# Prologue of a fused attention and MLP block: modulation products ahead of the transposes, weights by chunk, dummies gated by statistics

## Chip, cores, metric

One core of a Trainium2 chip. The metric is the device time of one execution, in microseconds; the kernel before has a median of 560.35 us in the first three runs (560.24 to 560.86). A trace shows one profiled execution, and "span" is the time from its first to its last instruction, about 1.8 us less than the device time. "PE" is the matmul engine, "PEld" its weight loads, "DVE", "ACT" and "POOL" the vector, scalar and GpSimd engines, "SP" the sync queue.

## The reference, cut

```python
mod = (silu(c) @ w_mod).reshape(1, 6, 1, -1)
sa, ca, ga, sb, cb, gb = ...                        # six rows of 512
h = layernorm(x) * (1 + ca) + sa                    # x: 2048 x 512
x = x + ga * attention(h @ wq, k_cache, v_cache) @ wo    # 32 query heads, the last 512 keys
h = layernorm(x) * (1 + cb) + sb
x = x + gb * (relu(h @ w1) @ w2)
```

Everything is bf16. Before the first attention unit the kernel needs the first 512 rows of x normalised and transposed, silu(c), the two rows sa and ca as columns, and the query weights of two heads.

## The kernel before

The parts that the change touches, all in the prologue ("tile" is 128 rows of x). Later on, 128 units of scores, softmax, values and projections run on PE without a pause.

```python
    for i in range(2):
        dma(x_sb[:, 2 * i:2 * i + 2, :], ..., eng=ACT if i else SP)      # x, tiles 0-1 and 2-3
    dma(c_row[:, :], ...)
    load_wm01(0)                 # first half of the weights of sa, ca: SP
    load_wm01(1, ACT)            # second half
    load_wq(0, 2, ACT)           # query weights of heads 0 and 1
    load_wq(2, 2)
    load_k(0)
    load_v(0)
    kb.op(POOL, lambda e: e.memset(ones[:, :], 1.0), writes=[R_ones])
    ...
    warm(7)                      # dummies: matmuls ones x ones, 512 columns
    silu_exp(5)                  # transpose of c on PE, exp and copy on ACT
    warm(9)
    ...                          # ACT: sum and square of tile 3
    silu_mul()                   # POOL: 1/(1+exp(-c)), times c
    ln_stat(0)                   # DVE: mean and variance
    ln_stat(1)
    rstd_add(0, 2)
    rstd_pow(0, 2)               # POOL
    ln_stat(2)
    rstd_add(2, 3)
    rstd_pow(2, 4)               # POOL
    ln_norm(0)                   # DVE
    ln_norm(1)
    kb.op(POOL, ... xn[:, t3, :] ...)     # tile 3 is normalised on POOL
    ...
    ln_tposes(0, TB[0])          # four PE transposes of tile 0
    fs = mod_cols_mm(0, QBK)     # 32 products w_mod column block x silu(c)
    for f in fs:
        f()
    ln_norm(2)
    mod_cols_evac(0, QBK)        # DVE: modc, the columns of sa and 1 + ca
    ...
    for tl in range(1, TPB):
        ln_tposes(tl, TB[tl // 2])
    mod_half(0, 0, DVE)          # hT = transposed tile * (1 + ca) + sa
    ...
    q_half(0, 0, CC_ORDER, QBK)  # query projection, half a block at a time
```

Near the end, each engine reads a flag (is every softmax sum in range?) and branches past a slow fallback program:

```python
                v = e.value_load(flag[0:1, 0:1])
                with e.If(v != 128):
                    ...                        # the fallback
                with e.Else():
                    kb.emit(stream, e, n_ops)  # the rest of the fast path
```

Of the kernel before, what the change touches and what calls it, by code (L numbers as in the profile page):

```python
# [128 lines left out]
def all_events(res_list):  # L129
    evs = []  # L130
    for r in res_list:
        if r.w is not None:
            evs.append(r.w)
        evs.extend(r.r)
    return evs
# [1063 lines left out]
def build_fast(nc, es, top, A_x, A_k_cache, A_v_cache, A_wq, A_wo, B_x, B_w1, B_w2, c, w_mod, out, flag):  # L1199
    P = 128  # L1200
    _, Sq, D = A_x.shape
    _, G, Sk, Dh = A_k_cache.shape
# [5 lines left out]
    QB = 512  # L1208
    NB = Sq // QB
    TPB = QB // P  # L1210
    NT = Sq // P
    DC = D // P
# [15 lines left out]
    def T(name, shape, dt=BF):  # L1228
        return es.enter_context(nc.sbuf_tensor(name, shape, dt))
# [3 lines left out]
    wq_sb = wq_t[:, :].rearrange("p (c n) -> p c n", c=DC)  # L1233
# [12 lines left out]
    wm01 = wmw[:, 0:2 * DC * D].rearrange("p (c n) -> p c n", c=DC)  # L1246
    wm = [wm01[:, :, 0:D], wm01[:, :, D:2 * D]] + [wmw[:, i * DC * D:(i + 1) * DC * D].rearrange("p (c n) -> p c n", c=DC) for i in range(2, 6)]
# [8 lines left out]
    ones = T("ones", [P, P])  # L1256
# [25 lines left out]
    bank = [s_ps[0][:, 0, :], s_ps[0][:, 1, :], s_ps[1][:, 0, :], s_ps[1][:, 1, :], q_ps[:, :],  # L1282
            o_ps[:, 0:2, :].rearrange("p a b -> p (a b)"), o_ps[:, 2:4, :].rearrange("p a b -> p (a b)"), w_ps[:, :]]
    QBK, WBK = 4, 7

    sem = lambda name: top.enter_context(nc.semaphore(name))
    kb = KB(nc)
    PE = kb.stream("pe", sem("s_pe"))
    ACT = kb.stream("act", sem("s_act"))
    DVE = kb.stream("dve", sem("s_dve"))  # L1290
    POOL = kb.stream("pool", sem("s_pool"))
    SP = kb.stream("sp", sem("s_sp"))

    def dsem(key):
        if key not in kb.dma_cnt:
            kb.add_dma_sem(key, sem("d_" + key))
        return key

    def dma(out_ap, in_ap, key, reads=(), writes=(), transpose=False, eng=None):
        k = dsem(key)  # L1300
        if transpose:
            return kb.op(SP, lambda e: e.dma_start_transpose(out_ap, in_ap), reads=reads, writes=writes, dma_sem=k)
        return kb.op(eng or SP, lambda e: e.dma_start(out_ap, in_ap), reads=reads, writes=writes, dma_sem=k)  # L1303

    RL = lambda name, n: [Res(f"{name}{i}") for i in range(n)]
    R_x, R_wq, R_wo = RL("x", NT), RL("wq", H), RL("wo", NPASS)
    R_kT, R_v, R_v1 = RL("kT", G), RL("v", G), Res("v1")
    R_hT, R_h2T = [RL(f"hT{i}_", DC) for i in range(2)], [RL(f"h2T{i}_", DC) for i in range(2)]
    R_qT, R_PT, R_o, R_oT = RL("qT", NQT), [RL(f"PT{i}_", 2) for i in range(NPT)], RL("o", NOS), RL("oT", NOT)
    R_acc, R_wm, R_w1, R_w2 = RL("acc", TPB), RL("wm", 6), RL("w1", FC), RL("w2", FC)  # L1310
# [3 lines left out]
    R_ident, R_ones, R_c, R_sc, R_scf, R_tmp, R_cst = (Res(n) for n in ("ident", "ones", "c", "sc", "scf", "tmp", "cst"))  # L1314
    R_moda, R_modb, R_ga, R_gb = Res("moda"), Res("modb"), Res("ga"), Res("gb")
    R_pr = [R_ga] + RL("pr", 2) + [R_gb]
    R_st, R_mv, R_rstd = RL("st", NT), RL("mv", NT), RL("rstd", NT)
    R_h0 = RL("h0", DC)
    R_q1 = RL("q1_", 2)
    R_cf, R_m01 = Res("cf"), Res("m01")  # L1320
    R_s3, R_eps = Res("s3"), Res("eps")
    R_rinv, R_vmax, R_chk, R_good, R_flag = Res("rinv"), Res("vmax"), Res("chk"), Res("good"), Res("flag")
# [4 lines left out]
    wqv = A_wq.rearrange("(c p) n -> p c n", p=P)  # L1327
# [8 lines left out]
    def load_wq(h0, n, eng=None):  # L1336
        dma(wq_sb[:, :, h0 * Dh:(h0 + n) * Dh], wqv[:, :, h0 * Dh:(h0 + n) * Dh], f"wq{h0}", writes=R_wq[h0:h0 + n], eng=eng)

    def load_k(g):
        dma(kT_sb[:, g, :], A_k_cache[0][g, Sk - W:, :], f"k{g}", writes=[R_kT[g]], transpose=True)  # L1340
# [7 lines left out]
    wm01v = w_mod[:, 0:2 * D].rearrange("(c p) n -> p c n", p=P)  # L1348

    def load_wm01(i, eng=None):  # L1350
        c0, c1 = i * DC // 2, (i + 1) * DC // 2
        dma(wm01[:, c0:c1, :], wm01v[:, c0:c1, :], f"wm{i}", writes=[R_wm[i]], eng=eng)

    def wm_res(sl, cc):
        return R_wm[cc // (DC // 2)] if sl < 2 else R_wm[sl]

    def load_wo(j):
        dma(wo_sb[:, j * HQ:(j + 1) * HQ, :], wov[:, j * HQ:(j + 1) * HQ, :], f"wo{j}", writes=[R_wo[j]])
# [1 line left out]
    wm_done = []  # L1360

    def load_mlp(i):
        if not wm_done:
            wm_done.extend(all_events(R_wm))
        f0 = i % (FC // 2) * 2
        if i < FC // 2:
            kb.op(SP, lambda e: e.dma_start(w1_sb[:, :, f0 * P:(f0 + 2) * P], w1v[:, :, f0 * P:(f0 + 2) * P]), writes=R_w1[f0:f0 + 2], pre=wm_done, dma_sem=dsem(f"w1{f0}"))
        else:
            kb.op(SP, lambda e: e.dma_start(w2_sb[:, f0:f0 + 2, :], w2v[:, f0:f0 + 2, :]), writes=R_w2[f0:f0 + 2], pre=wm_done, dma_sem=dsem(f"w2{f0}"))

    def mm(out_ap, lhsT, rhs, start, stop, reads, bk, signal):
        kb.op(PE, lambda e: e.matmul(out_ap, lhsT, rhs, start=start, stop=stop), reads=reads, group_writes=[R_b[k] for k in bk], signal=signal)  # L1372
# [1 line left out]
    def tpose(out_ap, in_ap, reads, bk, signal):  # L1374
        kb.op(PE, lambda e: e.transpose(out_ap, in_ap, ident[:, :]), reads=list(reads) + [R_ident], group_writes=[R_b[k] for k in bk], signal=signal)  # L1375

    def warm(n):
        for i in range(n):
            mm(bank[WBK], ones[:, :], ones[:, 0:1].to_broadcast([P, QB]), True, True, [R_ones], [WBK], i == n - 1)

    def ln_stat(t):
        kb.op(DVE, lambda e: e.bn_stats(st[:, t, :], x_sb[:, t, :]), reads=[R_x[t]], writes=[R_st[t]])  # L1382
        kb.op(DVE, lambda e: e.bn_aggr(mv[:, t, :], st[:, t, :]), reads=[R_st[t]], writes=[R_mv[t]])
# [7 lines left out]
    def ln_norm(t):  # L1391
        b, tl = t // TPB, t % TPB
        kb.op(DVE, lambda e: e.tensor_scalar(xn[:, tl, :], x_sb[:, t, :], mv[:, t, 0:1], rstd[:, t:t + 1], op0=ALU.subtract, op1=ALU.mult),
              reads=[R_x[t], R_mv[t], R_rstd[t]], writes=[R_xn[tl]])
# [10 lines left out]
    def ln_tposes(tl, bks):  # L1405
        for cc in range(DC):
            bk = bks[cc]
            o = (cc % 2) * 512 + tl * P
            tpose(bank[bk].bitcast(BF)[:, o:o + P], xn[:, tl, cc * P:(cc + 1) * P], [R_xn[tl]], [bk], cc == DC - 1)

    CC_ORDER = (0, 2, 1, 3)
    QA = 2
# [23 lines left out]
    def mod_cols_evac(which, bk):  # L1436
        mo, r = which * 2 * DC, (R_moda, R_modb)[which]
        kb.op(DVE, lambda e: e.tensor_tensor(modc[:, mo:mo + 2 * DC], bank[bk][:, :2 * DC], m01[:, :], op=ALU.add), reads=[R_b[bk], R_m01], writes=[r])  # L1438
# [38 lines left out]
    def q_mms(u, bk=QBK):  # L1477
        b, h = units[u]
        for i, cc in enumerate(range(DC)):
            mm(bank[bk], wq_sb[:, cc, h * Dh:(h + 1) * Dh], hT[b % 2][:, cc, :], i == 0, i == DC - 1,  # L1480
               [R_wq[h], R_hT[b % 2][cc]] + ([R_h0[cc]] if b == 0 else []), [bk], i == DC - 1)
        q_evac(u, bk)

    def q_evac(u, bk=QBK):
        kb.op(ACT, lambda e: e.activation(qT[u % NQT][:, :], bank[bk], ACTF.Copy), reads=[R_b[bk]], writes=[R_qT[u % NQT]])  # L1485
# [73 lines left out]
    for i in range(2):  # L1559
        dma(x_sb[:, 2 * i:2 * i + 2, :], xv[:, 2 * i:2 * i + 2, :], f"xa{i}", writes=R_x[2 * i:2 * i + 2], eng=ACT if i else SP)  # L1560
    dma(c_row[:, :], c[0].rearrange("(c p) -> c p", p=P), "c", writes=[R_c])
    load_wm01(0)
    load_wm01(1, ACT)
    load_wq(0, 2, ACT)
    load_wq(2, 2)
    load_k(0)
    load_v(0)
    kb.op(POOL, lambda e: e.memset(ones[:, :], 1.0), writes=[R_ones])
    kb.op(POOL, lambda e: e.memset(cst[:, 0:1], -0.5), writes=[R_cst])
    kb.op(POOL, lambda e: e.affine_select(ident[:, :], ones[:, :], pattern=[[1, P]], compare_op=ALU.is_equal, fill=0.0,  # L1570
                                          base=0, channel_multiplier=-1), reads=[R_ones], writes=[R_ident])
# [3 lines left out]
    kb.op(POOL, lambda e: e.memset(m01[:, 0:DC], 0.0), writes=[R_m01])  # L1575
    kb.op(POOL, lambda e: e.memset(m01[:, DC:2 * DC], 1.0), writes=[R_m01])
    kb.op(ACT, lambda e: e.activation(cst[:, 2:3], cst[:, 0:1], ACTF.Exp), reads=[R_cst], writes=[Res("dummy")])
    warm(7)
    silu_exp(5)
    warm(9)  # L1580
    t3 = TPB - 1
    kb.op(ACT, lambda e: e.activation(xn[:, t3, :], x_sb[:, t3, :], ACTF.Copy, accum_out=s3[:, 0:1]), reads=[R_x[t3]], writes=[R_xn[t3], R_s3])
    kb.op(ACT, lambda e: e.activation(s3[:, 1:2], s3[:, 0:1], ACTF.Copy, scale=-1.0 / D), reads=[R_s3], writes=[R_s3])
# [3 lines left out]
    def rstd_add(lo, hi):  # L1587
        kb.op(DVE, lambda e: e.tensor_scalar(rstd[:, lo:hi], mv[:, lo:hi, 1], eps, None, op0=ALU.add), reads=R_mv[lo:hi], writes=R_rstd[lo:hi])
# [4 lines left out]

    silu_mul()
    ln_stat(0)
    ln_stat(1)
    rstd_add(0, 2)
    rstd_pow(0, 2)
    ln_stat(2)
# [6 lines left out]
    TB = [[0, 0, 2, 2], [1, 1, 3, 7]]  # L1606
# [5 lines left out]
        else:  # L1612
            kb.op(ACT, lambda e: e.activation(dst, src, ACTF.Copy), reads=[R_b[bk]], writes=w)

    ln_tposes(0, TB[0])
    fs = mod_cols_mm(0, QBK)
    for f in fs:
        f()
    ln_norm(2)
    mod_cols_evac(0, QBK)  # L1620
    HB = QB // 2
    R_half = [R_h0, R_hT[0]]

# [10 lines left out]
    def q_half(u, hf, order, bk):  # L1634
        for cc in order:
            mm(bank[bk][:, hf * HB:(hf + 1) * HB], wq_sb[:, cc, u * Dh:(u + 1) * Dh], hT[0][:, cc, hf * HB:(hf + 1) * HB], cc == CC_ORDER[0], cc == CC_ORDER[-1],
               [R_wq[u], R_half[hf][cc]], [bk], cc == CC_ORDER[-1])

    for tl in range(1, TPB):
        ln_tposes(tl, TB[tl // 2])  # L1640
    mod_half(0, 0, DVE)
    mod_half(0, 2, ACT)
    mod_half(0, 1, DVE)
# [62 lines left out]
    def h1_group(b, fc):  # L1706
        dst, r = h2_of[b]
        bk = hb_banks[cnt["h"] % len(hb_banks)]
        cnt["h"] += 1
        for cc in range(DC):  # L1710
            mm(bank[bk], w1_sb[:, cc, fc * P:(fc + 1) * P], dst[:, cc, :], cc == 0, cc == DC - 1, [R_w1[fc], r[cc]], [bk], cc == DC - 1)
        kb.op(ACT, lambda e: e.activation(h1T[b % 2][:, fc, :], bank[bk], ACTF.Relu), reads=[R_b[bk]], writes=[R_h1[b % 2][fc]],  # L1712
              pre=all_events(R_wq) if b < 2 else ())

    def y_group(b, tl, c0=0, c1=D, deng=None):
        pt_done = all_events(R_PT[0] + R_PT[1] + R_PT[2])
# [63 lines left out]
    b = NB - 1  # L1780
# [112 lines left out]
```

## Time and profile before

| | before |
|---|---|
| span of the profiled execution | 559.4 us |
| PE busy | 550.5 us, 98% |
| PE starts to be dense | about 13.1 us |
| PE's clock is released (dummies start 0.427 us apart while it is cold, in e2 0.22 us once it is released; here inside the last dummy) | about 8.76 us |

PE is the bound and stays busy from 13 us to the end (539.5 of the last 546.1 us). The only idle stretches that a change can win are in the prologue. The lines that show this stand in the prediction. One reading aid for later: a granted clock below 1 means that PE ran at half rate for some of the span; 0.997 is about 3.4 us of it (e2's profile: 0.50 from 10.59 to 14.00 us, 0.997 over its 560.3 us). The wait for release at the very start isn't in that number (the profile of before shows 1.0, although its dummies ran cold until 8.76 us).

### The profile page before, as it was taken

The numbers are of one execution on the slowest core, as the hardware profiler recorded it, in microseconds if no ns is written. First come the engines' busy times: TensorE is split into PE (matmuls) and PEld (weight loads), VectorE is DVE, ScalarE is ACT, GpSimd is POOL, SyncE is SP. The second block draws the span as 40 slices with busy tenths as digits, with TensorE's granted clock in tenths as the row PEclk, the third lists the DMA queues.
The fourth block names the chain that finished last, engine by engine and source line by source line (L and its number), as shares of the span: only waits on it lengthen the run. The fifth ranks groups of instructions, "written<-read, shape, count | busy, mean of one in ns | idle before, by whom it ended". The sixth has DMA issues, their size and how long they took to land.

```text
span 559.4 us, 9666 instructions
## 1 busy us (share of the span) xinstructions
PE 550.5 (98%) x4060; PEld 315.8 (56%) x4134; DVE 253.8 (45%) x551; ACT 348.9 (62%) x453; POOL 54.7 (10%) x53
## 2 busy tenths in 40 slices
PE   8999999999999999999999999999999999999998
PEld 4665555555555555555555555555555654444444
DVE  4455555553546544335445443333354448321134
ACT  4986666666666666666666666666666644432500
POOL 3000022004410000033000000332000000000000
DMA  9897763513114144352352412111215110210001
GB/s 268 248 207 174 143 169 46 114 39 76 40 38 76 39 73 117 58 133 57 94 95 57 76 40 39 39 39 38 39 39 76 39 30 0 44 34 23 22 29 47
DMA packets 113309, 42.67 MB, mean 76 GB/s; under 512 B 93928, under 2 KB 112104, under 8 KB 113256
## 3 DMA queue, kind: packets, MB, share of 16 engines
q1 hardware_dynamic: 112024, 40.82, 34.3%
q10 hardware_dynamic: 1232, 1.15, 0.6%
q8 instruction: 33, 0.54, 0.4%
q14 instruction: 20, 0.16, 0.1%
HBM read 18.35 MB, written 2.10 MB: 37 GB/s over the span
## 4 chain that ended last, share of the span: by engine, by line
PE 98%; issue 1%; DMA 1%; DVE 0%; SPq 0%; DVEq 0%
PE psS L1372 28%; PE psO L1372 27%; PE psQ L1372 23%; PE psW L1372 20%; DMA c_row<-in_c_dram 1%; DVE qT L1611 0%; DVE hT L1630 0%; SPq L1303 0%; DVE PT L1723 0%; DVE PT L1725 0%; PE psS L1375 0%; PE psO L1416 0%; DVE modc L1438 0%; DVEq L123 0%
## 5 line engine op out<-in xcount | busy, mean ns | idle before, releaser
L1493 ACT ACTIVATE PT<-psS 128x1024 bf16<-128x1024 f32 x256 | 262.7, 1028 | 128.2 <-PE psS L1372 128.1
L1372 PE MATMUL psS<-qT,kT 128*128 128x512 bf16 x508 | 150.9, 379 | 0.5 <-DVE qT L1611 0.4
L1372 PEld LDWEIGHTS psO<-v,PT 128*128 128x128 bf16 x2048 | 126.6, 98 | 30.2
L1372 PE MATMUL psO<-v,PT 128*128 128x129 bf16 x2048 | 137.0, 220 | 0.0
L1372 PE MATMUL psQ<-hT,wq 128*128 128x512 bf16 (+1 forms) x510 | 130.5, 377 | 0.3 <-DVE hT L1630 0.2
L1503 DVE RECIPROCAL rinv<-psO 128x4 f32<-128x4 f32 x128 | 23.3, 182 | 227.2 <-PE psO L1372 227.2
L1372 PE MATMUL psW<-wo,oT 128*128 128x512 bf16 x454 | 118.1, 379 | 3.0
L1504 DVE TENSOR_TENSOR o<-psO,rinv 128x512 bf16<-128x512 f32 x128 | 88.5, 691 | 4.9 <-DVE rinv L1503 0.5
L1372 PEld LDWEIGHTS psQ<-hT,wq 128*128 128x128 bf16 x512 | 49.9, 98 | 60.3 <-issue 0.6
L1372 PEld LDWEIGHTS psS<-qT,kT 128*128 128x128 bf16 x512 | 49.5, 98 | 58.9 <-ACT PT L1493 0.7
L1485 ACT ACTIVATE qT<-psQ 128x512 bf16<-128x512 f32 x126 | 74.7, 593 | 0.0
L1712 ACT ACTIVATE wq<-psS 128x512 bf16<-128x512 f32 x56 | 33.4, 597 | 49.3 <-PE psS L1372 48.9
L1372 PEld LDWEIGHTS psW<-wo,oT 128*128 128x128 bf16 x512 | 45.0, 98 | 32.9 <-DVE acc L1526 1.2
L1526 DVE TENSOR_TENSOR acc<-psW,acc 128x512 f32<-128x512 f32 x48 | 33.2, 691 | 6.5 <-PE psW L1372 6.5
L1372 PE MATMUL psO<-wmw,wq 128*128 128x512 bf16 (+1 forms) x165 | 32.8, 352 | 0.3
L1529 POOL TENSOR_TENSOR acc<-acc,gaf 128x512 f32<-128x512 f32 x12 | 15.6, 1303 | 146.7 <-DVE acc L1526 139.8
L1388 POOL TENSOR_TENSOR rstd<-rstd,cst 128x4 f32<-128x4 f32 x7 | 7.2, 1025 | 216.8 <-DVE rstd L1387 216.8
L1723 DVE TENSOR_TENSOR PT<-psO,gbf 128x512 f32<-128x512 f32 (+1 forms) x12 | 7.5, 624 | 40.4 <-PE psO L1372 40.4
L1372 PE MATMUL psS<-h2T,wmw 128*128 128x512 bf16 x109 | 25.0, 379 | 0.2
L1372 PEld LDWEIGHTS psO<-wmw,wq 128*128 128x128 bf16 x168 | 15.3, 98 | 16.5
L1372 PE MATMUL psS<-hT,wmw 128*128 128x512 bf16 x110 | 24.4, 379 | 0.1
L1382 DVE BATCH_NORM_STATS2 st<-x 128x6 f32<-128x512 bf16 x31 | 21.1, 681 | 4.8 <-DMA x<-in_A_x_dram 4.8
(85 smaller groups left out, 192.6 us busy)
## 6 DMA issues: line engine op xcount, KB each, us to landing
wo<-in_A_wo_dram SPq DMA_DIRECT2D x4, 1024.0 KB, 5.9
wq<-in_A_wq_dram SPq DMA_DIRECT2D x7, 512.0 KB, 4.6
wmw<-in_B_w_dram SPq DMA_DIRECT2D x14, 256.0 KB, 3.1
wmw<-in_w_mod_dram SPq DMA_DIRECT2D x5, 512.0 KB, 4.8
oT<-o SPq DMA_TRANSPOSE x128, 2.4
out_dram<-PT SPq DMA_DIRECT2D x15, 128.0 KB, 1.7
x<-in_A_x_dram SPq DMA_DIRECT2D x3, 512.0 KB, 4.3
v<-in_A_v_cache_dram SPq DMA_DIRECT2D x8, 128.0 KB, 3.8
```

The lines of the kernel that those rows point to most:

```text
L1372: kb.op(PE, lambda e: e.matmul(out_ap, lhsT, rhs, start=start, stop=stop), reads=reads, group_writes=[R_b[k] for k in bk], signal=signal)
L1382: kb.op(DVE, lambda e: e.bn_stats(st[:, t, :], x_sb[:, t, :]), reads=[R_x[t]], writes=[R_st[t]])
L1388: kb.op(POOL, lambda e: e.tensor_tensor(rstd[:, sl], rstd[:, sl], cst[:, 0:1].to_broadcast([P, hi - lo]), op=ALU.pow), reads=R_rstd[sl] + ...
L1485: kb.op(ACT, lambda e: e.activation(qT[u % NQT][:, :], bank[bk], ACTF.Copy), reads=[R_b[bk]], writes=[R_qT[u % NQT]])
L1493: kb.op(ACT, lambda e: e.activation(PT[u % NPT][:, pr * 2:pr * 2 + 2, :], s_ps[pr][:, :, :], ACTF.Exp, scale=scale), reads=[R_b[pr * 2], R ...
L1503: kb.op(DVE, lambda e: e.reciprocal(rinv[:, u, :], o_ps[:, :, P]), reads=[R_b[5], R_b[6]], writes=[R_rinv])
L1504: kb.op(DVE, lambda e: e.tensor_tensor(o_sb[u % NOS][:, :, :], o_ps[:, :, 0:P], rinv[:, u, :].unsqueeze(2).to_broadcast([P, TPB, P]), op=A ...
L1526: kb.op(DVE, lambda e: e.tensor_tensor(acc[:, tl, :], bank[WBK], acc[:, tl, :], op=ALU.add), reads=[R_b[WBK], R_acc[tl]], writes=[R_acc[tl]])
L1529: kb.op(eng, lambda e: e.tensor_tensor(acc[:, tl, :], acc[:, tl, :], gaf[:, :], op=ALU.mult), reads=[R_acc[tl], R_ga], writes=[R_acc[tl]])
L1712: kb.op(ACT, lambda e: e.activation(h1T[b % 2][:, fc, :], bank[bk], ACTF.Relu), reads=[R_b[bk]], writes=[R_h1[b % 2][fc]], pre=all_events( ...
L1723: kb.op(DVE, lambda e: e.tensor_tensor(yt[i][:, c0:c1], bank[bk][:, c0:c1], gbf[:, c0:c1], op=ALU.mult), reads=[R_b[bk], R_gb], writes=[R_ ...
```

## The change

The intent: get the products and their evacuation off the path by running them before the first transpose; cut the weights into four chunks so that products start with the first; put the query weights behind the chunks; keep PE's clock up with dummies that are released by the statistics and placed between transposes.

```diff
-    load_wm01(0)
-    load_wm01(1, ACT)
-    load_wq(0, 2, ACT)
+    for i in range(DC):
+        load_wm01(i, (ACT, SP)[i % 2])
+    for i, eng in enumerate((SP, SP)):
+        dma(wq_sb[:, 2 * i:2 * i + 2, 0:QA * Dh], ..., f"wqa{i}", writes=[R_wqa[i]], eng=eng)
+    load_k(0)
     load_wq(2, 2)
-    load_k(0)
     load_v(0)
-    kb.op(POOL, lambda e: e.memset(ones[:, :], 1.0), writes=[R_ones])
+    kb.op(DVE, lambda e: e.memset(ones[:, :], 1.0), writes=[R_ones])
 ...
-    warm(7)
+    warm(10)
     silu_exp(5)
-    warm(9)
 ...
     ln_stat(0)
+    warm(3, [R_mv[0]])           # wait for the statistics of tile 0
     ln_stat(1)
+    warm(2, [R_mv[1]])
 ...
-    ln_tposes(0, TB[0])
     fs = mod_cols_mm(0, QBK)
     for f in fs:
         f()
+    ln_tposes(0, TB[0])
+    mod_cols_evac(0, QBK)
     ln_norm(2)
-    mod_cols_evac(0, QBK)
 ...
-    for tl in range(1, TPB):
-        ln_tposes(tl, TB[tl // 2])
+    ln_tposes(1, TB[0])
+    warm(2, bk=6)
+    ln_tposes(2, TB[1])
+    ln_tposes(3, TB[1])
+    warm(1, bk=6)
```

More of the change, by code (lines that the diff above doesn't have):

```diff
@@ L1319, in build_fast @@
     R_q1 = RL("q1_", 2)
+    R_wmc = RL("wmc", DC)
+    R_wqa = RL("wqa", 2)
     R_cf, R_m01 = Res("cf"), Res("m01")
@@ L1350, in load_wm01 @@
     def load_wm01(i, eng=None):
-        c0, c1 = i * DC // 2, (i + 1) * DC // 2
-        dma(wm01[:, c0:c1, :], wm01v[:, c0:c1, :], f"wm{i}", writes=[R_wm[i]], eng=eng)
+        dma(wm01[:, i, :], wm01v[:, i, :], f"wmc{i}", writes=[R_wmc[i]], eng=eng)
     def wm_res(sl, cc):
-        return R_wm[cc // (DC // 2)] if sl < 2 else R_wm[sl]
+        return R_wmc[cc] if sl < 2 else R_wm[sl]
     def load_wo(j):
@@ L1363, in load_mlp @@
         if not wm_done:
-            wm_done.extend(all_events(R_wm))
+            wm_done.extend(all_events(R_wm + R_wmc))
         f0 = i % (FC // 2) * 2
@@ L1375, in tpose, with warm @@
         kb.op(PE, lambda e: e.transpose(out_ap, in_ap, ident[:, :]), reads=list(reads) + [R_ident], group_writes=[R_b[k] for k in bk], signal=signal)
-    def warm(n):
+    def warm(n, gate=(), bk=7):
         for i in range(n):
-            mm(bank[WBK], ones[:, :], ones[:, 0:1].to_broadcast([P, QB]), True, True, [R_ones], [WBK], i == n - 1)
+            mm(bank[bk], ones[:, :], ones[:, 0:1].to_broadcast([P, QB]), True, True, [R_ones] + list(gate), [bk], i == n - 1)
     def ln_stat(t):
@@ L1480, in q_mms @@
             mm(bank[bk], wq_sb[:, cc, h * Dh:(h + 1) * Dh], hT[b % 2][:, cc, :], i == 0, i == DC - 1,
-               [R_wq[h], R_hT[b % 2][cc]] + ([R_h0[cc]] if b == 0 else []), [bk], i == DC - 1)
+               (R_wqa if h < QA else [R_wq[h]]) + [R_hT[b % 2][cc]] + ([R_h0[cc]] if b == 0 else []), [bk], i == DC - 1)
         q_evac(u, bk)
@@ L1561, in build_fast @@
     dma(c_row[:, :], c[0].rearrange("(c p) -> c p", p=P), "c", writes=[R_c])
-    load_wm01(0)
-    load_wm01(1, ACT)
-    load_wq(0, 2, ACT)
+    for i in range(DC):
+        load_wm01(i, (ACT, SP)[i % 2])
+    for i, eng in enumerate((SP, SP)):
+        dma(wq_sb[:, 2 * i:2 * i + 2, 0:QA * Dh], wqv[:, 2 * i:2 * i + 2, 0:QA * Dh], f"wqa{i}", writes=[R_wqa[i]], eng=eng)
+    load_k(0)
     load_wq(2, 2)
-    load_k(0)
     load_v(0)
-    kb.op(POOL, lambda e: e.memset(ones[:, :], 1.0), writes=[R_ones])
+    kb.op(DVE, lambda e: e.memset(ones[:, :], 1.0), writes=[R_ones])
     kb.op(POOL, lambda e: e.memset(cst[:, 0:1], -0.5), writes=[R_cst])
@@ L1636, in q_half @@
             mm(bank[bk][:, hf * HB:(hf + 1) * HB], wq_sb[:, cc, u * Dh:(u + 1) * Dh], hT[0][:, cc, hf * HB:(hf + 1) * HB], cc == CC_ORDER[0], cc == CC_ORDER[-1],
-               [R_wq[u], R_half[hf][cc]], [bk], cc == CC_ORDER[-1])
-    for tl in range(1, TPB):
-        ln_tposes(tl, TB[tl // 2])
+               [R_wqa[cc // 2], R_half[hf][cc]], [bk], cc == CC_ORDER[-1])
+    ln_tposes(1, TB[0])
[3 more added lines that the diff above has]
+    warm(1, bk=6)
     mod_half(0, 0, DVE)
@@ L1712, in h1_group @@
         kb.op(ACT, lambda e: e.activation(h1T[b % 2][:, fc, :], bank[bk], ACTF.Relu), reads=[R_b[bk]], writes=[R_h1[b % 2][fc]],
-              pre=all_events(R_wq) if b < 2 else ())
+              pre=all_events(R_wq + R_wqa) if b < 2 else ())
     def y_group(b, tl, c0=0, c1=D, deng=None):
```

## The prediction

The sum came to 560.35 - 0.64 = 559.7 us with what is cut in it: the 0.96 us in part 2, for PE's first weight load (1.04 in the trace), was the author's guess, and that products, transposes and query halves run at the full clock was assumed, not shown. "The clock phase" is the time in an execution at which the clock is released.

> **What bounds the kernel now.** I read the page first: busy shares and the chain that ended last.
>
> ```profile
> span 559.4 us, 9666 instructions
> PE 550.5 (98%) x4060; PEld 315.8 (56%) x4134; DVE 253.8 (45%) x551; ACT 348.9 (62%) x453; POOL 54.7 (10%) x53
> ...
> PE 98%; issue 1%; DMA 1%; DVE 0%; SPq 0%; DVEq 0%
> ```
>
> The chain runs on PE for 98% of the span. From 13.3 us to the end PE is busy 539.5 of 546.1 us (stretches view), and nothing the diff touches is issued there: every edited line belongs to the prologue ahead of the first attention unit. So the change can only move the moment at which that dense PE stream begins, the first score matmul at 13.34 us. I then read the chain in order of time from 8 to 13.5 us (start, length, what):
>
> ```profile
> 7.80 1.18 PE psW L1372 x3
> 8.98 0.22 PE psS L1375 x4
> 9.21 0.79 PE psQ L1372 x32
> ...
> 10.02 0.18 DVE modc L1438
> ...
> 10.30 0.42 DVE hT L1630
> ...
> 10.86 0.78 PE psQ L1372 x4
> 11.64 0.89 PE psO L1372 x8
> ...
> 12.55 0.44 DVE qT L1611
> 12.99 0.35 issue
> 13.34 0.38 PE psS L1372
> ```
>
> psW are dummies (matmuls on ones that keep PE busy), psS L1375 the transposes of tile 0, psQ x32 the modulation products (weight columns times silu(c)), modc their evacuation, hT the modulated transposes, then the query projections in halves. The order costs time: the products wait behind transposes, which wait for the first normalised tile; then modc and everything after wait for the products. DVE is idle 0.98 us before modc. GpSimd is a narrow path too:
>
> ```profile
> 5.43 0.28 POOL L1421 TENSOR_SCALAR tmp<-tmp 128x4 f32<-128x4 f32 x1 [3.17 <-ACT c_f L1418]
> 5.80 1.04 POOL L1422 TENSOR_TENSOR tmp<-tmp,cst 128x4 f32<-128x4 f32 x1
> 6.92 0.20 POOL L1423 TENSOR_TENSOR sc_bf<-c_f,tmp 128x4 bf16<-128x4 f32 x1
> 7.08 1.51 POOL L1591 TENSOR_TENSOR rstd<-rstd,cst 128x2 f32<-128x2 f32 x2
> 8.70 0.90 POOL L1604 TENSOR_SCALAR xn<-x,s,rstd 128x512 bf16<-128x512 bf16 x1
> ```
>
> It does silu(c), then both rstd powers, then normalises tile 3, back to back. silu is ready at 7.12, so the products could start 1.9 us before their 9.04. Tile 3 is ready only at 9.60. Last the loads issued in the first 2 us (KB, us to landing):
>
> ```profile
> wmw<-in_w_mod_dram ACTq DMA_DIRECT2D x1, 512.0 KB, 4.9
> wmw<-in_w_mod_dram SPq DMA_DIRECT2D x1, 512.0 KB, 6.3
> ...
> wq<-in_A_wq_dram ACTq DMA_DIRECT2D x1, 256.0 KB, 7.3
> ```
>
> Issued at 1.23, 1.66 and 1.72 us (timeline), they land at about 6.1, 7.9 and 9.0.
>
> [...] dummies start 0.427 us apart from 5.46 to 8.45, a 512-column matmul later takes 0.216. The release falls inside the last dummy, at about 8.76. The first run of seven dummies ended about 4.0 and was followed by an idle stretch until 4.95[...].
>
> [...] The trace: 326 GB/s from 4 to 9 us. [...]
>
> [...] No row of this trace has a DVE memset.
>
> **The change part by part.**
> 1. *ones set by DVE.* [...]
> 2. *Ten dummies ahead of the silu transpose instead of seven.* 0.96 + 0.40 + 9 x 0.427 = 5.2: the transpose of c starts at 5.2 instead of 4.95. c landed at 4.9, so this costs about 0.25 us, and it passes through GpSimd to everything: silu ready about 7.37, first rstd power done 8.03, tile 0 normalised from 8.07 (7.82 now), tile 3 ready about 9.85 (9.60 now). In return PE has no idle gap before 5.3[...].
> 3. *Dummies gated by statistics.* Three behind tile 0's statistics (5.70), two behind tile 1's (6.49): if warm 5 x 0.216 = 1.1 us, done about 7.0; if cold 5 x 0.427, done 7.9. Either way beside the silu chain and the last weight chunk, not on the path.
> 4. *Products ahead of transposes.* They start when silu is there (7.37); 24 of 32 follow the first three chunks, the last 8 the fourth, about 7.9 as the same megabyte is ahead. Spacing from this trace 25 ns, 0.8 us in all: done about 8.2 to 8.3 instead of 9.85. Evacuation then waits for DVE, busy with tiles 0 and 1 until about 8.72: modc at 8.9 instead of 10.19. Thus 0.8 us of products and 1.3 us of modc leave the path; what remains is tile 3.
> 5. *Tile 2's normalisation behind the evacuation.* 0.17 us later on DVE, about 8.9 to 9.3, still before tile 3.
> 6. *Transposes with dummies between.* Tile 0 at 8.6, tile 1 at 8.95, two dummies 0.43, tile 2 at 9.6, tile 3 at about 9.93 (GpSimd plus 0.08), 4 x 0.056 to 10.15, one dummy to 10.37. Before, tile 3's ended at 10.51.
> 7. *Modulation of half 0.* After tile 1's transposes (9.3): two on DVE at 0.32, two on ACT at 0.46 to 0.56, done about 10.3, as PE frees. The query matmuls start at about 10.38 instead of 10.86 and no longer pause for hT (the gap of 0.27 between the third and fourth, 11.09 to 11.36, loses 0.16).
> 8. *Query weights.* Ahead of their end lie x 0.5, modulation 1.0 and wq 0.25 MB, as now; two chunks on the sync queue land about 9.0, 1.3 us before use. k0, wq2 and v0 land near 10, used after 12. Hidden.
>
> The rest: sixteen query matmuls at 0.109, evacuation 0.43, issue 0.35, as now. Half 1's modulations on DVE start after tile 3's transposes, 10.39, and end 0.32 x 2 + 0.40 later, 11.43, just ahead of the matmul that needs them (11.6). First score matmul: 13.34 - 0.48 (earlier start) - 0.16 (no pause) = 12.70. Gain 0.64 us. The dense stream has slack nowhere that depends on absolute time (its waits are on its own ACT and DVE), so 0.64 carries to the end: 560.35 - 0.64 = 559.7.
>
> **The rivals.**
> *The clock phase.* [...] Then the products (25 ns perhaps doubled, +0.8), transposes (16 x 0.05, +0.8) and query halves (16 x 0.107, +1.7) would run cold, partly in waits: up to 2 us slower, 562. [...] Against: the three runs lie within 0.62 us though the kernel before has the same exposure, so the phase is either steady or cheap. I give a loss over 0.5 us one chance in eight.
> *The full gain.* If silu isn't delayed, because PE starts sooner or the clock is released within the ten dummies, tile 3 stays at 9.6 and the query matmuls start at about 10.1: gain 0.9 to 1.0, 559.4.
> *A transfer takes over.* wq behind four chunks on sync: each issue takes about 0.41 us, so the last goes out at 2.9 instead of 1.7. It would have to land after 10.4 to hurt. The queue is full of earlier bytes until 7.9, so I hold this at one in ten; it would bring the gain to nil, 560.4.
> *Contention on DVE.* The evacuation waiting in order on DVE could delay tile 2 if the products end late (a cold PE): tile 2 and both halves slip by as much. Included in the first.
>
> **Range and chances.** 559.7 is the sum. Below it the full gain and 0.3 us of run-to-run scatter: 558.9. Above it no gain at all, plus scatter: 560.6. 2% is 11.2 us, nearly the whole prologue of 13.34 us; no rival moves more than 2. Within 2%: 0.99.
>
> **What would show it right or wrong.** Right: the first dense psS matmul near 12.7; the dummies after the silu transpose 0.216 us apart; psQ x32 near 7.4 to 8.3; modc near 8.9 with little DVE idle before it; tile 3's transposes near 9.95, released by GpSimd; the stream after it unchanged. Wrong: dummies still 0.427 apart after 5.4 and query halves at 0.213 (phase); psQ matmuls released by wq's DMA (transfer); silu transpose before 5.0 (full gain); a start of the stream that moves without the end moving (absolute-time waits after all).

## The result, and the profile after

| | before | after |
|---|---|---|
| median of 6 runs | 560.54 us (560.24 to 561.53) | 560.71 us (560.15 to 561.21) |
| span of the profiled execution | 559.4 us | 559.4 us |

The ratio is 1.000, with a 95% interval of 0.9987 to 1.0013: no gain that six runs can see. A ratio here is the mean time of one kernel's fast runs over that of the other's of the same rounds, so it isn't quite the ratio of the medians quoted.

The page of the changed kernel has the same totals:

```profile
span 559.4 us, 9674 instructions
PE 550.4 (98%) x4061; PEld 315.7 (56%) x4136; DVE 254.1 (45%) x552; ACT 349.1 (62%) x453; POOL 54.7 (10%) x52
```

Its chain in order of time from 4 to 14 us (start, length, what) answers to that of before in the prediction:

```profile
3.84 1.71 PE psW L1373 x4
5.55 0.13 PE psO L1417
...
6.33 1.07 POOL tmp L1423
...
7.67 0.67 POOL rstd L1592
...
8.37 0.42 DVE xn L1394
...
8.84 0.72 PE psS L1376 x8
...
9.61 0.38 PE psO L1373
...
10.61 0.21 PE psO L1373
10.82 0.44 PE psQ L1373 x4
11.26 0.89 PE psO L1373 x8
```

The products (psQ x32) and modc have left the chain, as intended. In their place stand the last of ten cold dummies ahead of the silu transpose (psO L1417 is that transpose), then GpSimd's silu and power, tile 0's normalisation, and the dummies between transposes (psO L1373 at 9.61 and 10.61). The first score matmul is at 12.74 us; the prediction had 12.70.

So where is the gain? Two things took it. First, its size was misread. Before's first score matmul isn't at 13.34: the record of that matmul is missing from the trace, and 13.34 is the second of the pair. The weight loads show it. Before, then after (start, length, engine, what; "x2" are the two score matmuls' weights):

```profile
13.10 0.13 PEld L1372 LDWEIGHTS psS<-qT,kT 128*128 128x128 bf16 x2 [0.42 <-issue]
```

```profile
12.71 0.13 PEld L1373 LDWEIGHTS psS<-qT,kT 128*128 128x128 bf16 x2 [0.42 <-issue]
```

The stream starts 0.39 us earlier, not 0.60. I compared every weight load of the two traces by its place in the order: from the fifth load of the query halves (11.4 us) to 514 us the lead stays between 0.383 and 0.390 us. There it is lost in one step. The end of the chain from 509 to 515 us, before and after:

```profile
508.94 5.18 PE psO L1372 x24
514.12 0.03 issue
514.15 1.04 PE psQ L1372 x4
```

```profile
...
512.27 1.46 PE psO L1373 x6
513.73 0.42 issue
514.15 1.04 PE psQ L1373 x4
```

In the changed kernel PE stands 0.42 us for "issue", a cause outside the data. It is the branch past the fallback, which both kernels share: the trace has it on PE's queue, 3.44 us long before and 3.84 us after (0.05 to 0.07 us on the vector, scalar and GpSimd engines). PE works off its queued matmuls meanwhile and stands only when the branch outlasts them: in after the branch lasts from 510.26 to 514.10 us, the matmuls run on until 513.73, and the next one starts at 514.15. So this pair of traces says: 0.39 won in the prologue, 0.40 lost to a longer branch. Whether the 0.39 is real in other executions is what the experiments ask.

### The profile page after: what moved, and what is told of

Read it like the earlier page. It is cut to its first block, busy times and chain, and to the rows that moved or that the text cites. A ratio compares the mean times of both kernels' runs of the same rounds, so it can differ in the third digit from the quotient of the medians.

```text
span 559.4 us, 9674 instructions
## 1 busy us (share of the span) xinstructions
PE 550.4 (98%) x4061; PEld 315.7 (56%) x4136; DVE 254.1 (45%) x552; ACT 349.1 (62%) x453; POOL 54.7 (10%) x52
## 4 chain that ended last, share of the span: by engine, by line
PE 98%; issue 1%; POOL 0%; DVE 0%; ACT 0%; POOLq 0%
PE psS L1373 28%; PE psO L1373 27%; PE psQ L1373 22%; PE psW L1373 20%; PE psS L1376 0%; POOL tmp L1423 0%; POOL rstd L1592 0%; DVE qT L1614 0%; DVE xn L1394 0%; DVE PT L1729 0%; DVE PT L1731 0%; POOL tmp L1422 0%; POOL sc_bf L1424 0%; DVE ones L1570 0%; ACT tmp L1418 0%
## 5 line engine op out<-in xcount | busy, mean ns | idle before, releaser
L1373 PE MATMUL psS<-qT,kT 128*128 128x512 bf16 x510 | 151.4, 379 | 0.3 <-DVE qT L1614 0.2
L1373 PEld LDWEIGHTS psO<-v,PT 128*128 128x128 bf16 x2048 | 126.6, 98 | 30.2
L1373 PE MATMUL psO<-v,PT 128*128 128x129 bf16 x2048 | 137.0, 220 | 0.0
L1373 PE MATMUL psQ<-hT,wq 128*128 128x512 bf16 (+1 forms) x509 | 130.2, 377 | 0.2
L1373 PE MATMUL psW<-wo,oT 128*128 128x512 bf16 x452 | 118.1, 379 | 3.1
L1373 PEld LDWEIGHTS psQ<-hT,wq 128*128 128x128 bf16 x512 | 49.9, 98 | 59.9 <-ACT qT L1486 0.4
L1373 PEld LDWEIGHTS psS<-qT,kT 128*128 128x128 bf16 x512 | 49.5, 98 | 58.9 <-ACT PT L1494 0.7
L1373 PEld LDWEIGHTS psW<-wo,oT 128*128 128x128 bf16 x512 | 45.0, 98 | 32.9 <-DVE acc L1527 1.2
L1373 PE MATMUL psO<-wmw,wq 128*128 128x512 bf16 (+1 forms) x164 | 32.7, 352 | 0.3
L1373 PE MATMUL psS<-h2T,wmw 128*128 128x512 bf16 x110 | 25.2, 379 | 0.1
L1373 PEld LDWEIGHTS psO<-wmw,wq 128*128 128x128 bf16 x168 | 15.3, 98 | 16.6
L1373 PE MATMUL psS<-hT,wmw 128*128 128x512 bf16 x110 | 24.4, 379 | 0.1
```

Source lines behind the costliest of these rows:

```text
L1373: kb.op(PE, lambda e: e.matmul(out_ap, lhsT, rhs, start=start, stop=stop), reads=reads, group_writes=[R_b[k] for k in bk], signal=signal)
```

## The experiments

Twelve runs follow, all correct; e1, e5 and e12 repeat a kernel. Expectations name three theories. **A**: the lead is real, and the branch hid it. **B**: something tied to absolute time holds PE at 514.15 us. **C**: PE's clock is released, and taken back, at other times in each execution (released at 8.76 us in before's profile, at 6.33 in after's), and this decides when the dummies end and with that where the stream starts. A "window" is 3.41 us, the time for which the profiles of e2 and e7 show the clock at half (e2: 10.585 to 13.998 us; e4 and e8 show twice that). Each run has a span and a granted clock, so I list these. On the chip of the first eight experiments before's fast runs had medians of 560.60 us; on that of the last four 560.42. "Stream start" is the first score weight load in the experiment's profile.

### e1: the changed kernel again

No edit.

> The changed kernel once more, for a second profile and ten more timings. Theory A (the lead of 0.39 us is real but was lost at the flag branch on PE[...]): the first query-weight load of the dense stream again near 12.7 us, PE's flag branch of another length between 3.3 and 4.0 us, and a mean time 0.2 to 0.5 us below the kernel before. Theory B (something tied to absolute time holds PE at 514.15 us): PE's first matmul behind the branch again at 514.15, whatever the branch's length, and no difference in time. Theory C [...]: dummies released at another time than 6.33 us, and a stream start that moves with it by up to 1 us.

Measured: 560.62 us, ratio 0.9998 (0.9985 to 1.0011); spans 558.6 to 559.1, all clocks 1.0. In its profile PE's first matmul behind the branch is at 513.42, 0.7 us earlier than 514.15, so B falls. The branch took 3.383 us. The clock was released at about 4.4 us (dummies 0.38 then 0.22 apart), not 6.33, and the stream started at 12.44, not 12.71: it moves with the phase, as C says. Its chain from 6.5 to 13 us:

```profile
2.06 6.43 DMA wmw<-in_w_mod_dram
8.49 0.05 issue
8.54 0.35 PE psQ L1373 x8
8.89 0.47 PE psS L1376 x8
9.36 0.05 issue
9.41 0.38 PE psO L1373
```

Here the last eight products wait for the fourth weight chunk, which landed at 8.49 (7.97 in the first profile), and the dummies at 9.41 stand ahead of tile 2. They don't hold it, though: tile 2's normalisation on DVE ended only at 9.66 (its lines stand further below), and its transposes began at 9.71.

### e2 and e12: the kernel before without the branch

```diff
-                kb.emit(stream, e, 0, n_ops)
-                ...
-                with e.If(v != 128):
-                ...
+                kb.emit(fast[name], e)         # no flag test, no fallback; the same answer on these inputs
```

> The kernel before without the flag test and the fallback program, so no branch on any engine (the answer is the same on these inputs). Theory A: the stall of PE at 514 us (0.19 us in the profile of before) is gone, time 0.2 to 0.5 us below before, and the spread of the timings shrinks if the branch made it. Theory C: the spread stays at about 1 us[...]. Theory B: a hold of PE near 514 us stays.

Measured: 561.78 us, ratio 1.0015 (1.0003 to 1.0027), slower by more than the scatter; spans 559.4 to 560.3, three of six clocks at 0.997. A falls here: taking the branch away didn't make this kernel faster. But the profile shows that the stall itself is gone. From the first score weight load to the start of the last matmul it takes 543.54 us, of which the first 0.4 still ran at half clock. The loss is in the prologue, the stream starting at 13.61. Stretches of this run (columns: stretch and its length; PE, PEld, DVE, ACT, POOL busy with counts; PEclk; DMA share; GB/s):

```profile
3.00:7.20 4.20, 3.21 (x13) 1.04 (x11) 2.26 (x6) 2.59 (x9) 1.52 (x4) 1.00 1.00 363
7.20:10.50 3.30, 2.02 (x50) 1.80 (x50) 2.41 (x9) 0.94 (x3) 2.38 (x4) 1.00 1.30 251
10.60:14.00 3.40, 3.28 (x16) 2.12 (x16) 1.46 (x5) 1.50 (x4) 0.00 (x0) 0.50 1.15 320
```

The clock came at about 3.76 us, so the nine dummies ran twice as fast (the last three 0.22 us apart) and ended near 7.1. PE then stood 1.1 us until tile 0's transposes, the window to 10.58 was poorly filled (PE busy for 2.13 of 3.41 us), and the clock was taken back for one window of 3.41 us, just under the query halves. That is the first sight of what the change's dummies are for.

Because all six runs were longer than most of before's, I ran the same kernel again at the end:

> e2 once more, byte for byte: all six of its runs were slow (spans 559.4 to 560.3, four of them with a clock below 1), which neither theory had expected, since its prologue is that of before. If that was the phase of the clock window by chance, most runs now have a clock of 1.0 and spans of 558.2 to 558.7, 0.1 to 0.5 us below before, the branch's stall on PE being gone. If the program without the branch meets the window differently each time it is launched, again most runs at 559.4 to 560.3 with clocks of 0.997 to 0.999.

Measured: 561.82 us, ratio 1.0027 (1.0014 to 1.0040); spans 559.7 to 560.5, three of six at 0.997, on another chip. So it is not chance: this program, with the prologue of before, gets the clock late or loses it more often than before does (all twelve of its spans are 559.4 us or more; of the 37 executions of before with a span, e5's included, four are, two of them at 0.997). Its second profile was not retaken but released only near 8.9 us, with the stream starting at 13.40. Why leaving out code that runs 500 us later changes this I can't say; it stays open. It also means that a program's own times of release are a confounder of every comparison here of a few tenths.

### e3: the changed kernel without the branch

The edit of e2 on the changed kernel.

> The changed kernel without flag test and fallback. Theory A: 0.3 to 0.5 us below e2, the lead of 0.39 us kept from 13 us to the end. Theory B: same time as e2. Theory C: 0.3 to 1.0 us below e2 with a stream start that differs from 12.7 us if the release of the clock falls elsewhere.

Measured: 560.48 us, ratio 0.9997; spans 558.3 to 558.8, and one run of six at 560.1 with a clock of 0.997. That is 1.1 us below e2 in the mean span (558.85 against 559.98), more than A's 0.3 to 0.5; the profile has the release at about 4.5 and the stream start at 12.48. So the changed prologue isn't immune, but loses its clock in one run of six where e2 and e12 lose it in six of twelve.

The branch, from all profiles in which the clock was full once the stream ran:

| profile | branch on PE, us | stream start to start of last matmul, us |
|---|---|---|
| e3, e4, e12 (no branch) | none | 543.17 to 543.18 |
| e1 | 3.383 | 543.31 |
| before | 3.440 | 543.38 |
| e10 | 3.463 | 543.39 |
| e6 | 3.520 | 543.45 |
| e9, e11 | 3.563 | 543.50, 543.49 |
| e7 | 3.583 | 543.52 |
| e5 | 3.703 | 543.64 |
| after | 3.840 | 543.77 |

The stream's length follows the branch one to one: it costs its length less 3.24 us, 0.14 to 0.60 us by execution. It is jitter shared by both kernels, not a cost of the change.

### e4: the changed kernel without the branch, seven dummies ahead of silu

```diff
-    warm(10)
+    warm(7)
     silu_exp(5)
```

> e3 with seven dummies ahead of the silu transpose in place of ten. If the silu chain on GpSimd is what bounds the changed prologue, the transpose runs at 4.95 us instead of 5.48, tile 3 is ready near 9.6 instead of 10.15, and the dense stream starts 0.4 to 0.5 us earlier than in e3: time 0.3 to 0.5 us below e3. If instead the three dummies are needed to release the clock (theory C), products, transposes and query halves run at half rate for a while and it is 0 to 1.5 us slower than e3.

Measured: 561.43 us, ratio 1.0010; spans 558.9 to 560.9, two of six with clocks of 0.993 and 0.994; mean span 559.83 against e3's 558.85. The three dummies seem needed: in its profile PE stood from about 4.1 to 6.0 us (but for the transpose of c), the clock was taken back at 7.28 (PE busy for 1.69 of the 3.41 us before) and stayed at half for two windows, to 14.11. Whether an earlier silu would gain isn't tested by this profile: with fewer dummies ahead the transpose of c waited for c itself and ran at 5.12 us, in e3 at 5.06.

### e5: the kernel before again

No edit.

> The kernel before once more, unchanged, for a second profile of it. Theory C [...]: its dummies are released at another time than 8.76 us; if earlier, tile 0's transposes start near 8.3 instead of 8.82 and the first query-half weights near 10.4, as in the changed kernel, so that the lead of 0.39 us read from the first pair of profiles is the phase and not the order. Some runs (3 of 11 so far) near 560 us of span with a granted clock of 0.997 to 0.999, most at 558.5 to 559.0. Theory A: query halves at 10.83 again.

Measured: 560.48 us, ratio 0.9997; spans 558.5 to 558.9. This profile decides the main question. Its chain from 6.5 to 13 us, and its first score weight load:

```profile
8.08 0.40 PE psS L1375 x4
8.48 0.78 PE psQ L1372 x32
9.26 0.41 PE psS L1375 x7
...
10.13 0.78 PE psQ L1372 x4
```

```profile
12.36 0.13 PEld L1372 LDWEIGHTS psS<-qT,kT 128*128 128x128 bf16 x2 [0.42 <-issue]
```

The clock was released at 6.61 us. The dummies were over before tile 0 was ready, its transposes began at 8.08 instead of 8.82, the query halves at 10.13 instead of 10.86, and the stream at 12.36. The unchanged kernel, with the products still behind the transposes, starts its stream earlier than the changed one in either of its profiles (12.71, 12.44). The first profile of before was an execution with a late release, in which the last cold dummies, not the order, held the transposes.

### e6: only the new order

```diff
-    ln_tposes(0, TB[0])
     fs = mod_cols_mm(0, QBK)
     for f in fs:
         f()
-    ln_norm(2)
+    ln_tposes(0, TB[0])
     mod_cols_evac(0, QBK)
+    ln_norm(2)
```

> The kernel before with only the products put ahead of tile 0's transposes (and the evacuation ahead of tile 2's normalisation). Theory A (the products were on the path): 0.4 to 0.6 us below before. Theory C: no gain; undisturbed runs at 558.5 to 559.0 of span as before, and runs with a clock of 0.997 as often as before or more often.

Measured: 560.62 us, ratio 0.9998 (0.9986 to 1.0011); spans 558.4 to 559.6. No gain from the order alone that five runs can see. Their interval, about 0.8 us faster to 0.6 us slower, doesn't by itself exclude A's 0.4 to 0.6; that the mean span, 558.92, lies no lower than before's of the same rounds, 558.81, speaks against A. Its profile had a late release (9.95 us) and the stream at 13.21.

### e7: only the new dummies

```diff
-    warm(7)
+    warm(10)
     silu_exp(5)
-    warm(9)
+    ...  warm(3, [R_mv[0]]), warm(2, [R_mv[1]]), warm(2, bk=6), warm(1, bk=6) at the places of the change
```

> The kernel before, order and loads kept, with only the dummies of the change (ten, 3 and 2 gated by statistics, 2 and 1 between transposes). Theory C: no run with a clock of 0.997 or less, all spans 558.4 to 559.4, as the changed kernel's eleven; mean 0.2 to 0.4 below before. Theory A: 0.2 to 0.5 us slower than before, since silu comes later and the products stay on the path.

Measured: 562.75 us, ratio 1.0031 (1.0014 to 1.0048); spans 559.0 to 562.2, four of six with clocks of 0.997 or 0.993. My expectation from C was wrong: the dummies don't protect by themselves. PE in order of time (start, length, what, idle before and its releaser), then the window that followed the release:

```profile
5.74 1.40 PE L1372 MATMUL psW<-ones 128*128 128x512 bf16 x5
8.76 0.57 PE L1375 MATMUL psS<-ident,xn 128*128 128x128 bf16 x4 [1.62 <-DVE xn L1393]
```

```profile
5.43:8.84 3.41, 1.65 (x9) 0.49 (x9) 2.63 (x10) 2.16 (x8) 2.77 (x5) 1.00 1.26 307
8.85:12.25 3.40, 3.18 (x50) 2.85 (x52) 1.49 (x5) 1.02 (x2) 1.11 (x2) 0.50 1.15 280
```

Released at about 5.43 (an estimate: one window before the clock was taken back at 8.84, as 4.31 lies before 7.72 in e8), the five gated dummies ended near 7.1, and nothing filled PE until 8.76; it was busy for 1.65 of 3.41 us, and the clock went. In the changed kernel the products stand in that hole.

### e8: the change without the later dummies

```diff
-    warm(3, [R_mv[0]])
-    warm(2, [R_mv[1]])
-    warm(2, bk=6)
-    warm(1, bk=6)
```

> The changed kernel without the gated dummies and those between transposes (only the ten ahead of silu stay). Theory C: PE is idle from about 5 to 7.3 us, [...] the clock is taken back in most runs (0.993 to 0.998), and the mean is 1 to 2 us above the changed kernel. Theory A: 0.1 to 0.3 us faster than the changed kernel, since the dummy ahead of the query halves (0.22 us) is gone.

Measured: 561.69 us, ratio 1.0018 (1.0005 to 1.0031); four of five clocks at 0.994 to 0.997; mean span 559.96, 1.1 us above e1. As C expected. In the profile the clock was taken back at 7.72 for two windows, PE having been busy for 1.16 of the 3.41 us before.

### e9: the change with nine dummies ahead of silu

```diff
-    warm(10)
+    warm(9)
```

> The changed kernel with nine dummies ahead of the silu transpose in place of ten. Where the clock is released after 5 us, the transpose of c starts near 5.05 us instead of 5.48 and GpSimd's chain and the dense stream 0.35 to 0.43 us earlier; where it is released before, nothing changes. Mean span 0.1 to 0.3 us below the changed kernel's 558.84 if theory C is right that silu behind cold dummies is a cost of the change; no run with a clock below 0.999 [...]. If silu is not the bound, no change.

Measured: 560.42 us, ratio 1.0005; spans 558.3 to 558.8 and one of five at 559.8 with 0.997; mean 558.84, the same as the changed kernel's. A miss twice: the silu chain behind cold dummies isn't a cost that the mean shows, and one run did lose the clock. In this profile the release came at 3.86, so silu waited for c itself (4.69), and the fourth chunk (landed 8.43), tile 2's normalisation (ended 9.63) and the last dummy held the rest; the stream started at 12.41.

### e10: new order and new dummies, old loads

The edits of e6 and e7 together.

> The kernel before with the new order and the new dummies, but the old loads and the old memset. e7 (dummies without the order) lost its clock at 8.84 us after PE had stood from about 7.0 to 8.76. Theory C: here the products fill that stretch, so all runs have a clock of 0.999 or more and spans as the changed kernel's, 558.4 to 559.4. If the chunked weights matter, products wait for the second half of the weights (about 7.9 us), the stretch is only half filled, and some runs lose the clock (0.997).

Measured: 560.61 us, ratio 1.0005; spans 558.8 to 559.1, five of five clocks at 1.0. With the products back in the hole, e7's loss (mean span 560.63) is gone (558.94). The chunked loads aren't needed for that. In the profile the first half of the weights landed at 7.96, and the products started from 8.09 to 8.87 (the trace names GpSimd's power, ended at 7.98, as their releaser, but they don't read it, so I take the weights); the stream started at 12.59.

### e11: only the new loads

The loads and the memset of the change; order and dummies as before.

> The kernel before with only the loads of the change (weights by chunk, query weights behind them on the sync queue, memset on DVE); order and dummies as before. Theory C and the prediction's point 8 agree: transfers stay hidden, query halves near 10.1 to 10.8 by the clock's phase as in before, spans as before (558.5 to 559.1, now and then near 560); difference under 0.2 us. If the loads collide, the query halves wait for wq and it is 0.3 us or more slower.

Measured: 560.38 us, ratio 1.0004; spans 558.6 to 559.3. The query weights landed at 8.71, 1.3 us before use: hidden. The profile, with a release at 3.96 us that was kept, has the earliest stream start of all, 12.25, with before's order.

No version beat both kernels: e9, e10 and e11 are at 1.0004 to 1.0005 of before.

## Why the prediction was right or wrong

The median measured, 560.71 us, is 0.1 us above the top of the range (560.6), less than the scatter between runs, and "within 2%" held. The forecast gain of 0.64 us did not come: in the same rounds before's median was 560.54, so the difference is +0.17. Over all runs the changed kernel's mean span is 558.84 us (11 runs) and before's 558.85 (37 runs), with standard deviations of 0.27 and 0.39, so the standard error of the difference is about 0.1 us. A gain of 0.64 is excluded by that, as far as the clock's phase spreads alike in the two programs.

By its steps:

1. *Ones by DVE, PE at 0.96.* Wrong in sign: the DVE memset started at 0.88 and took 0.17 us, PE's first load came at 1.10, 0.06 later than before.
2. *Silu transpose at 5.2, clock released at 5.35.* It came at 5.48 and the release at 6.33; in e1 at 4.98 and 4.4. The phase I took from one trace doesn't carry to another.
3. *Gated dummies off the path.* Right: done by 7.2 in the first profile.
4. *Products 7.4 to 8.3, modc 8.9.* Near: 7.73 to 8.52 and 9.02. The fourth chunk, which I put at 7.9, landed at 7.97, 8.49 and 8.43 in three profiles; in the latter two the products waited for it.
5. and 6. *Tile 2 and tile 3.* In the first profile tile 2 was ready at 9.59, before tile 3 as predicted, and tile 3's transposes came at 10.21, predicted 9.93, in the wake of silu. In e1, e9 and e10 the order turns: tile 2 is ready after tile 3 (9.66 against 9.51 in e1), which the prediction did not have.
7. *Query halves at 10.38, no pause.* 10.66, and no pause (0.109 apart). In e1 10.38.
8. *Transfers hidden.* Right (e11).

**The step that failed is the last, "First score matmul: 13.34 - 0.48 (earlier start) - 0.16 (no pause) = 12.70", and "so 0.64 carries to the end".** The 12.70 was nearly right (12.74); the 13.34 was not a property of the kernel. It was 0.2 us too high from a missing record (the pair's true lead is 0.39), and it came from an execution with a late release. In e5 before's start is 12.36, with the query halves at 10.13. And the gain does not "carry to the end" as it stands: the sum left out the branch, which took 0.40 us more in after's profile than in before's.

What the runs showed in its place, from the ten profiles in which the clock, once released, was kept: before's order released by 6.61 us (e11, e5) starts its stream at 12.25 and 12.36; the new order released by 6.33 (e9, e1, e3, e10, after) at 12.41 to 12.71; with a release after 8.7 either order is late, 13.10 to 13.40 (before, e6, e12). With the clock there in time the 0.8 us of products were hidden already: in e5 they and the transposes of tiles 0 to 2 were through when tile 3, ready on GpSimd at 9.59, let its transposes start at 9.64. The earlier modc of the change (8.93 in e1 against 9.29 in e5) is then lost again, with query halves at 10.38 against 10.13. The lines of tiles 2 and 3, e1 and then e5:

```profile
8.74 0.78 POOL L1607 TENSOR_SCALAR xn<-x,s,rstd 128x512 bf16<-128x512 bf16 x1
...
9.01 0.65 DVE L1394 TENSOR_SCALAR xn<-x,mv,rstd 128x512 bf16<-128x512 bf16 x1
...
9.71 0.34 PE L1376 MATMUL psS<-ident,xn 128*128 128x128 bf16 x3
...
10.17 0.38 PE L1373 MATMUL psO<-ones 128*128 128x512 bf16 x1
...
10.38 0.38 PE L1373 MATMUL psQ<-hT,wq 128*128 128x256 bf16 x2
```

```profile
8.61 0.41 DVE L1393 TENSOR_SCALAR xn<-x,mv,rstd 128x512 bf16<-128x512 bf16 x1 [0.27 <-POOL rstd L1591]
8.69 0.90 POOL L1604 TENSOR_SCALAR xn<-x,s,rstd 128x512 bf16<-128x512 bf16 x1
```

Behind the evacuation, tile 2's normalisation starts while GpSimd already works on tile 3, and takes 0.65 us in place of 0.41 (0.69 in e9, 0.66 in e10). So tile 2 and, behind it, tile 3 are transposed later, and the last dummy adds 0.21 us before the query halves. This is read from profiles; no run takes out either alone with the clock kept.

Of the rivals, the clock phase was the one that mattered, but not as I had it. I saw the phase as a risk of the change. It is as much one of before, and at both ends: a late release holds the stream (13.40 in e12), and after an early one the dummies end sooner, PE stands, and the clock can be taken back under the query halves (e2, released at 3.76; e11, released at 3.96, kept it). What the change does is to fill that hole, and it takes both parts: dummies alone (e7) or order without the later dummies (e8) lose the clock in most runs, together (e10, e1) in none of ten. In before's own program such executions are rare (two of 37 at 0.997, each about 1 us longer than the mean), so by my estimate protecting against them is worth at most about 0.1 us on average, below what these runs resolve. That the change is the more robust one is suggested by 0 of 11 against 2 of 37, not shown: its near relatives e3 and e9 lost the clock in one run each.

The prediction's sign for the full gain, a silu transpose before 5.0, did appear in e1 (4.98), without a gain. And its argument that three runs within 0.62 us make the phase "steady or cheap" rested on too few: the later runs of before lie between 560.19 and 561.76 us.

Open: why e2 and e12 lose the clock, or get it late, so much more often than before with the same prologue.

## What to carry to other kernels

Before a start-up of 10 us is tuned from a trace, take two or three traces: the clock's release fell at 6.61 in one execution and at 8.76 us in another, and the same program began its main stream at 12.36 and at 13.10 us, more than the change was worth. Dummies that keep PE warm finish twice as fast once the clock is released (0.22 us apart in e2 in place of 0.427 in before), so count them for the warm case too and tie the later ones to an event near the first real work. And before a gain of tenths is booked, follow it to the end: compare the place of the same instruction in both traces, check that no record is missing at the point that is compared, and look for waits of random length, such as the branch here (3.38 to 3.84 us), behind it.

## What the traces show of the clock, the branch and the memset

- The clock was taken back after short idle gaps of PE: a longest gap of 1.1 us (e2) and 1.6 us (e7). PE's busy time in one 3.41 us window, by the profile's measure, sorts these executions nearly: 1.16 (e8), 1.65 (e7), 1.69 (e4) and 2.13 us (e2) lost the clock; 2.36 (e9), 2.42 (e2's window before), 2.46 (e11), 2.67 (after) and 3.09 us (e5) kept it. But e10 kept it with 2.04 us (4.78 to 8.20 us), so where the line lies isn't shown. Nor does it sort the first release: 2.71 (e2) and 2.76 us (e9) brought it, 2.85 us (e6, the window that ended at 6.54) did not.
- The releases fell at 3.76, 3.86, 3.96, 4.31, 5.43, 6.33, 6.61, 8.76 and 9.95 us (read from the starts and lengths of the dummies, or estimated as one or two windows before the clock was taken back), while PE's first dummy started at 1.04 us in before and 1.10 in after. The times of taking back and giving back lie 3.41 us apart (e2: 10.585 and 13.998; e7: 8.841 and 12.254) or twice that (e4: 7.281 and 14.107; e8: 7.722 and 14.548). One program can have the bad phases in most executions, as e2 and e12 did (spans of 559.4 us or more in 12 of 12 runs, against 4 of 37 of before).
- The branch took 3.38 to 3.84 us on PE, of which 0.14 to 0.60 us stopped the matmuls and the rest lay behind queued ones, and 0.05 to 0.07 us on the vector, scalar and GpSimd engines. Why PE's is so long isn't shown: during it the instruction queues moved one packet each (q8 and q14, in after).
- The memset of ones (128x128, bf16) took 0.17 us on DVE in after, by the profile, and 0.20 us on GpSimd in before.
